# A linear-attention and low-rank mixer kernel: the order and banks of its half-size products, its x, u and kv units, and where attention stands between them

## The chip, the cores and the metric

One core of one Trainium2 chip. The metric is the device time of one execution in microseconds. In the text, TensorE (PE) multiplies, VectorE (DVE), ScalarE (ACT) and GpSimd (POOL) work on elements, and SyncE (SP) issues DMAs; POOL issues some as well.

## The reference

Eight samples of 8 heads, 576 positions and 64 features go through a linear attention; its output x (576 x 512 per sample) goes through a low-rank mixing over positions and a two-layer network.

```python
r = maximum(x, 0)                       # for q and for k, then
phi = concatenate([r * cos(theta), r * sin(theta)])        # theta by position
kv, z = einsum('bhsf,bhsd->bhfd', k_p, v), sum(k_p, axis=2)
x = einsum('bhsf,bhfd->bhsd', q_p, kv) / (einsum('bhsf,bhf->bhs', q_p, z)[..., None] + 1e-06)
h = x.transpose(0, 2, 1) @ U @ V        # rank 32, over positions
u = x + h.transpose(0, 2, 1)
out = u + maximum(u @ w_ch1, 0.0) @ w_ch2                  # 512 -> 2048 -> 512
```

## The kernel before

A sample's 576 positions are four blocks of 128 (c = 0 to 3) and a tail of 64 (c = 4); the tails of two samples share one block ("tail" units). All instructions are put in order by hand: a list `slots` holds 274 units, and a table `todo` holds what is put behind each of them, in order. Each engine works through its own instructions in that order.

The slots, for pairs of samples (even e, odd o):
- first layer: 16 units `g1_main` (L541: four matmuls of 512 columns into one of three banks tagged "g"; L550: ScalarE's relu into `hid`). Sample 0 starts at slot 0, then samples 1 to 7 at 32, 70, 100, 138, 168, 206, 236. For odd samples four `g1_tail` units (L561, L568) follow.
- second layer: for sample 0 four plain products (L601, L609). For samples 1 to 7, 14 units `w_part` (L708): seven products of half the size, each of 16 matmuls of 256 columns in two half-steps. They need sums of blocks of `hid` ("S" forms, L684: four forms, each made in two halves on VectorE, the third in place in `hid`) and of w_ch2 ("T" forms, `w2_form`, L660: eight VectorE instructions, made once). The results go into two banks, "oA" and "oB", in turns. Between them: ScalarE's cast of the first product into `w_sum` (L108), VectorE's add to it (L722), three GpSimd adds of `w_sum` and u into the output tiles `o_sb` (L722), VectorE's adds, and the stores (L575).
- behind odd samples four `g2_tail` units (L625, L634), whose output goes through the same ring of two `o_sb` buffers.

PSUM has eight banks: "g" three, "X" two (x units), "T" one, "oA" and "oB" one each.

Attention of sample b is put behind slots, relative to a slot w(b) in the table PLAN:
- features: `q_prep`, `k_prep` (L267 on VectorE, L265 on ScalarE): for each block a cos and a sin instruction, 20 per sample, all on one engine for most samples; `v_prep` (L110, GpSimd) casts v.
- `qtr_dma` (L344, L349): SyncE's transposing DMAs of q, three per sample.
- `kv_unit` (L301): 20 matmuls and a VectorE cast, twice; `x_unit` (L408): 8 matmuls, then VectorE's rec (L365, L366) and product (L418), five times, all in the two banks "X"; `A_unit` (L433, L439) with a cast on VectorE; `u_unit` (L453, L456; L460 the VectorE add), four or five times; the bank of kv, A and u is chosen by `spare`.
- `utr_dma` (L476, L482): transposing DMAs of u into uT, which the sample's first layer reads.
- `loads` of sample b + 1's q, k and v (L74, L81, L87) on SyncE, into single buffers.

```python
PLAN = {
    2: (45, -15, V_, V_, -10, (-5, -4, -4)),   # w, features at, engines for q and k, q transposes, loads
    3: (64, -11, V_, A_, -6, (7, 7, 12)),
    4: (100, -20, V_, V_, -12, (-6, -6, -6)),
    5: (134, -20, A_, A_, -13, (-7, -7, -7)),
    6: (168, -20, V_, V_, -12, (-6, -6, -6)),
    7: (202, -20, A_, A_, -13, ()),
}
```

Of the kernel before, what the change touches and what calls it, by code (L numbers as in the profile page):

```python
# [17 lines left out]
def kernel(  # L18
# [36 lines left out]
    ps = ctx.enter_context(tc.tile_pool(name="ps", bufs=1, space=bass.MemoryType.PSUM))  # L55

# [176 lines left out]
    G3, T1, OA, OB = ("g", 3), ("T", 1), ("oA", 1), ("oB", 1)  # L233
    turn = [0]

    def O2():
        turn[0] += 1
        return (OB, OA)[turn[0] % 2]

# [53 lines left out]
    def kv_unit(b, hg, tag, bufs, eng=None):  # L293
        if b not in kv_sb:
            kv_sb[b] = pool.tile([P, H, E], BF16, tag="kv", bufs=2, name="kv")
        acc = ps.tile([P, 4, E], FP32, tag=tag, bufs=bufs, name="kv_ps")
# [11 lines left out]
        cast(eng or V_, kv_sb[b][:, hg * 4 : hg * 4 + 4, :], acc)  # L308

    def qT_alloc(b):  # L310
        if b not in q_pT:
            q_pT[b] = pool.tile([P, 4, H, P], BF16, tag="q_pT", bufs=2, name="q_pT")

    def qtr_unit(b, c, h0=0, h1=H, eng=None, tag="T", bufs=1):
        qT_alloc(b)
        t_ps = ps.tile([P, H, P], BF16, tag=tag, bufs=bufs, name="t_ps")
# [51 lines left out]
    def den_unit(b, h0, h1, tag, bufs):  # L368
        n = h1 - h0
        d_ps = ps.tile([P, 5, n], FP32, tag=tag, bufs=bufs, name="d_ps")  # L370
# [12 lines left out]

    def xh_unit(b, c, h0, h1, rec, tag, bufs):
# [3 lines left out]
        acc = ps.tile([P, n, D], FP32, tag=tag, bufs=bufs, name="xh_ps")  # L388
# [12 lines left out]
    def x_unit(b, c, tag, bufs):  # L401
# [3 lines left out]
        acc = ps.tile([P, 2, 512], FP32, tag=tag, bufs=bufs, name="x_ps")  # L405
# [22 lines left out]
    def A_unit(b, tag, bufs, eng=None, n0=0, n1=DM, a_ps=None):  # L428
        if a_ps is None:
            a_ps = ps.tile([P, DM], FP32, tag=tag, bufs=bufs, name="a_ps")  # L430
# [15 lines left out]
    def u_unit(b, c, tag, bufs):  # L446
# [4 lines left out]
        va = ps.tile([P, DM], FP32, tag=tag, bufs=bufs, name="va_ps")  # L451
        if c < 4:
            nc.tensor.matmul(out=va, lhsT=V_bf[:, c, :], rhs=A_of(b), start=True, stop=True)  # L453
        else:
# [7 lines left out]
            op=ALU.add,  # L462
        )
# [22 lines left out]
    def uTd_open(b, d, tag, bufs, t=None):  # L486
        uT_alloc(b)
        if t is None:
            t = ps.tile([P, 4, P], FP32, tag=tag, bufs=bufs, name="uT_ps")
# [105 lines left out]
    def g2_part(cc, part):  # L595
        if part == 0:
            tag, bufs = G3 if cc >= 2 else O2()
            o_ps[cc] = ps.tile([P, DM], FP32, tag=tag, bufs=bufs, name="o_ps")
# [14 lines left out]
    def g2_tail(pr, part):  # L613
        last = pr == NPAIR - 1
        if part == 0 or last and part == 3:
            tag, bufs = OB if part == 0 else OA
            o_ps[pr] = ps.tile([P, DM], FP32, tag=tag, bufs=bufs, name="ot_ps")
# [34 lines left out]
    def w2_form(n, half):  # L652
# [7 lines left out]
        V_.tensor_tensor(out=T[n][:, r, :], in0=a, in1=b_, op=op)  # L660
# [25 lines left out]
    w_ps, w_sum = {}, {}  # L686

    def w_part(b, n):
        step, half = divmod(n, 2)
        if n == 0:  # L690
            w_ps[b, 0] = ps.tile([P, 2, HD], FP32, tag="oA", bufs=1, name="wa_ps")
        if n == 2:
            w_ps[b, 1] = ps.tile([P, 2, HD], FP32, tag="oB", bufs=1, name="wb_ps")
        bank = w_ps[b, step % 2]
        lhs, rhs = (
            (lambda: hid_block(b, 0, 0), w2_block(0, 0)),
            (lambda: s_forms[b, 2], T[1]),
            (lambda: hid_block(b, 1, 0), w2_block(1, 0)),
            (lambda: s_forms[b, 1], T[0]),
            (lambda: s_forms[b, 3], T[2]),  # L700
            (lambda: s_forms[b, 4], w2_block(1, 1)),
            (lambda: hid_block(b, 1, 1), T[3]),
        )[step]
        lhs = lhs()
        opens = step in (0, 1, 3, 4)
        for k_ in range(half * 4, half * 4 + 4):
            for g in range(2):
                nc.tensor.matmul(  # L708
                    out=bank[:, g, :], lhsT=lhs[:, k_, g * P : g * P + P], rhs=rhs[:, k_, :],
# [3 lines left out]
        if n < 2:  # L713
            for f in ((1, 2), (4, 3))[n]:
                hid_form(b, f, 1)
# [8 lines left out]
        if step == 0:  # L724
            w_sum[b] = pool.tile([P, 2, HD], FP32, tag="w_sum", bufs=1, name="w_sum")
            cast(A_, w_sum[b], bank)
        elif step == 1:
            w = w_sum[b]
            o0, o1 = o_alloc(b, 0), o_alloc(b, 1)
            add(V_, w, w, bank)  # L730
# [3 lines left out]
        elif step == 2:  # L734
            o0 = o_sb[b, 0]
            add(V_, o0[:, :, lo], u[:, 0:2, lo], bank)
        elif step == 3 or step == 4:
            o = o_sb[b, 1][:, :, hi]
            add(V_, o, o, bank)
        elif step == 5:  # L740
            o = o_sb[b, 0][:, :, hi]
            add(V_, o, o, bank)
            store(store_eng(b), b, 0, o_sb[b, 0])
        else:
            o = o_sb[b, 1][:, :, lo]
            add(V_, o, o, bank)
# [21 lines left out]
    def first_units(b):  # L768
        starts[b] = len(slots)
        lay([lambda j=j: g1_main(b, j) for j in range(NJ)], False)  # L770
        if b > 0:
            for i in range(4):
                beside.setdefault(starts[b] + 9 + i, []).append(
                    lambda i=i: hid_form(b, (1, 2, 4, 3)[i], 0)
                )
# [21 lines left out]
    def spare(at):  # L797
        if second[at]:
            return T1 if not all(second[at : at + 2]) else G3
        return T1 if any(second[at : at + 3]) else O2()  # L800

    QORD = (4, 0, 1, 2, 3)
    PLAN = {
        2: (45, -15, V_, V_, -10, (-5, -4, -4)),
        3: (64, -11, V_, A_, -6, (7, 7, 12)),
        4: (100, -20, V_, V_, -12, (-6, -6, -6)),
        5: (134, -20, A_, A_, -13, (-7, -7, -7)),
        6: (168, -20, V_, V_, -12, (-6, -6, -6)),
        7: (202, -20, A_, A_, -13, ()),
    }  # L810

    def attention_plan(b):

        plan = []
        w, f_at, q_eng, k_eng, qtr, lo = PLAN[b]

        def put(at, f, *a, tag=False):
            if tag:
                a = a + spare(w + at)
            plan.append((w + at, lambda: f(b, *a)))  # L820

        for n, c in enumerate(QORD):
            if b == 3:
                put(f_at + 2 * n, q_prep, c, (q_eng, q_eng))
                put(n - 8, k_prep, c, (k_eng, k_eng))
                put(-3 if n > 2 else n - 10, v_prep, 0, H, (c,), (A_ if n > 2 else G_,))
                continue
            put(f_at + n, q_prep, c, (q_eng, q_eng))
            put(f_at + 6 + n, k_prep, c, (k_eng, k_eng))
            put(f_at + 3 + (3 * n) // 2, v_prep, 0, H, (c,), (G_,))  # L830
        for n, (c0, c1) in enumerate(((4, 5), (0, 2), (2, 4))):
            put(qtr + 2 * n, qtr_dma, c0, c1)
        put(0, kv_unit, 0, tag=True)
        put(2, kv_unit, 1, tag=True)
        for n, c in enumerate(ORD):
            put(4 + 2 * n, x_unit, c, "X", 1)
        put(14, A_unit, tag=True)
        odd = b % 2 == 1
        for n, c in enumerate((4, 0, 1, 2, 3) if odd else (0, 1, 2, 3)):
            put(16 + n, u_unit, c, tag=True)  # L840
        if odd:
            put(18, utr_dma, 4, 5)
        put(18 + odd, utr_dma, 0, 2)
        put(20 + odd, utr_dma, 2, 4)
        for at, t in zip(lo, loads(b + 1) if lo else ()):
            plan.append((w + at, t))
# [16 lines left out]
    def xh_mm(b, c, h0, tag, bufs):  # L863
        acc = ps.tile([P, 4, D], FP32, tag=tag, bufs=bufs, name="xh_ps")
# [46 lines left out]
    def first_chain(b):  # L911
# [30 lines left out]
        a_ps = ps.tile([P, DM], FP32, tag=ao[0], bufs=ao[1], name="a_ps")  # L942
        a_mm(b, a_ps, 0, 256, range(5))
        cast(A_, A_of(b)[:, 0:256], a_ps[:, 0:256])
        for tag, bufs in (T1, O2()):
            t.insert(-1, ps.tile([P, 4, P], FP32, tag=tag, bufs=bufs, name="uT_ps"))
# [17 lines left out]
    for c in TL:  # L964
        tg = G3 if c < 3 else O2()
        t_q.append(ps.tile([P, H, P], BF16, tag=tg[0], bufs=tg[1], name="t_ps"))
# [69 lines left out]
    for n, c in enumerate(ORD):  # L1036
        at((32, 42, 43, 44, 45)[n], lambda c=c: u_unit(1, c, *O2()))
# [5 lines left out]
    for n in range(4):  # L1043
        for half in range(2):
            todo.setdefault(33 + 2 * n + half, []).append(
                lambda n=n, half=half: w2_form(n, half)
            )
# [44 lines left out]
```

## Time and profile before

| what | value |
|---|---|
| three runs | 341.31 us median, 338.14 to 346.68 |
| the profiled execution | 341.27 us, its span 338.8 us |
| granted TensorE clock, mean | 0.967 |
| TensorE busy | 304.1 us, 90% of the span |
| VectorE, ScalarE, GpSimd busy | 205.7, 139.5, 71.6 us |

An engine's busy time is the union of its instructions. A wait line reads "engine, line and tile that waited <- what it waited for: total us, times, longest". A window line gives the stretch, its length, the busy time and number of instructions, the granted clock as a share of full speed, the DMA engines' busy share and GB/s. A timeline line gives start, length, engine, line, operation, tiles, shapes, count, and in brackets the idle time before it.

### The profile page before, as it was taken

What the parts mean: (1) busy time and instruction counts of PE and PEld (TensorE: products, weight loads), DVE (VectorE), ACT (ScalarE), POOL (GpSimd) and SP (SyncE); (2) the same over time, 40 slices, a digit from 0 to 9 for tenths busy, and PEclk for the clock granted to TensorE, in tenths of its full rate; (3) what the DMA queues carried; (4) which work ended last, traced back from release to release, by engine and by line L of the source; (5) the groups of instructions that cost most, each with busy time, mean ns of one, the idle gap of its engine ahead of it and who ended that gap; (6) DMA issues with size and microseconds to landing.
All of it is one profiled execution on the core that took longest, in us unless ns stands there. A gap on an engine that the chain in (4) does not pass through costs nothing. (4 is left out here: it accounts for less than half of the span.)

```text
span 338.8 us, 6435 instructions
## 1 busy us (share of the span) xinstructions
PE 304.1 (90%) x2641; PEld 194.1 (57%) x2641; DVE 205.7 (61%) x419; ACT 139.5 (41%) x236; POOL 71.6 (21%) x105
## 2 busy tenths in 40 slices
PE   6999999975969499799997979779997999999995
PEld 2675455432947243585486634566466754874883
DVE  4778734998499248963863246982764357633341
ACT  3835720550580045104598035203689145127500
POOL 8500300400050105061304140051123210300030
PEclk9799999995999989899999989999999999999998
DMA  7999799689218994599239970299818510330004
GB/s 220 354 233 280 129 232 273 209 166 301 77 18 120 260 277 122 102 235 327 83 57 163 314 244 2 46 174 285 258 21 137 160 43 12 67 122 4 2 0 155
DMA packets 85279, 53.25 MB, mean 157 GB/s; under 512 B 54019, under 2 KB 82979, under 8 KB 85251
## 3 DMA queue, kind: packets, MB, share of 16 engines
q1 hardware_dynamic: 78802, 41.40, 49.7%
q0 software_dynamic: 6368, 11.43, 13.3%
q8 instruction: 20, 0.33, 0.4%
q14 instruction: 9, 0.07, 0.1%
q10 hardware_dynamic: 80, 0.03, 0.0%
HBM read 36.86 MB, written 9.44 MB: 137 GB/s over the span
## 5 line engine op out<-in xcount | busy, mean ns | idle before, releaser
L550 ACT ACTIVATE hid<-g_ps 128x512 bf16<-128x512 f32 x128 | 76.2, 597 | 140.4 <-PE g_ps L541 102.6
L541 PE MATMUL g_ps<-uT,w_bf 128*128 128x512 bf16 x512 | 125.6, 389 | 4.4 <-DMA uT<-u_bf 4.4
L541 PEld LDWEIGHTS <-w_bf 128*128 128x128 bf16 x512 | 47.9, 99 | 66.3 <-issue 14.1
L708 PEld LDWEIGHTS <-hid 128*128 128x128 bf16 x448 | 44.2, 99 | 14.4 <-issue 7.9
L722 POOL TENSOR_TENSOR o_sb<-w_sum,u_bf 128x512 f32<-128x512 f32 x21 | 26.8, 1297 | 114.2 <-DVE w_sum L722 102.8
L708 PEld LDWEIGHTS <-S 128*128 128x128 bf16 x336 | 32.8, 98 | 8.5 <-DVE S L684 2.4
L708 PE MATMUL wa_ps<-w_bf,hid 128*128 128x256 bf16 x224 | 28.7, 283 | 3.9 <-ACT w_sum L108 3.8
L110 POOL CAST v_ext<-vst 128x512 bf16<-128x512 f32 (+1 forms) x28 | 19.8, 733 | 55.7 <-DMA vst<-in_v_dram 55.7
L708 PE MATMUL wb_ps<-T,S 128*128 128x256 bf16 x224 | 27.0, 273 | 3.8 <-DVE S L684 2.1
L708 PE MATMUL wa_ps<-T,hid 128*128 128x256 bf16 x224 | 26.9, 273 | 0.4 <-DVE o_sb L722 0.3
L460 DVE TENSOR_TENSOR u_bf<-x_bf,va_ps 128x512 bf16<-128x512 bf16 x32 | 21.7, 681 | 8.8 <-PE va_ps L453 8.8
L365 DVE TENSOR_SCALAR rec<-x_ps 128x8 f32<-128x8 f32 (+1 forms) x35 | 5.7, 164 | 32.4 <-PE x_ps L408 32.4
L453 PE MATMUL va_ps<-A_sb,V_bf 128*128 128x512 bf16 x32 | 12.6, 393 | 8.8 <-DVE u_bf L460 7.8
L418 DVE TENSOR_TENSOR x_bf<-x_ps,rec 128x512 bf16<-128x512 f32 x28 | 19.4, 691 | 1.0
L110 DVE CAST kv<-kv_ps 128x260 bf16<-128x260 f32 x15 | 6.4, 428 | 18.4 <-PE kv_ps L301 18.4
L575 POOL DMA_DIRECT2D out_dram<-o_sb x12 | 7.6, 631 | 47.2 <-DVE o_sb L609 24.9
L408 PEld LDWEIGHTS <-q_pT 128*128 128x128 bf16 x224 | 10.9, 101 | 11.4 <-DMA vst<-in_v_dram 2.5
L722 DVE TENSOR_TENSOR o_sb<-o_sb,wb_ps 128x512 f32<-128x512 f32 x14 | 9.6, 686 | 12.1 <-PE wb_ps L708 11.2
L722 DVE TENSOR_TENSOR o_sb<-o_sb,wa_ps 128x512 f32<-128x512 f32 x14 | 9.6, 685 | 12.1 <-PE wa_ps L708 12.1
L684 DVE TENSOR_TENSOR S<-hid 128x1024 bf16<-128x1024 bf16 x14 | 9.5, 682 | 10.9 <-ACT hid L550 10.9
L561 PE MATMUL gt_ps<-uT_tl,w_bf 128*128 128x128 bf16 x256 | 16.1, 219 | 0.0
L561 PEld LDWEIGHTS <-w_bf 128*128 128x128 bf16 x256 | 15.1, 98 | 1.4
(143 smaller groups left out, 401.6 us busy)
## 6 DMA issues: line engine op xcount, KB each, us to landing
qst<-in_q_dram SPq DMA_DIRECT2D x14, 512.0 KB, 6.4
kst<-in_k_dram SPq DMA_DIRECT2D x14, 512.0 KB, 8.3
vst<-in_v_dram SPq DMA_DIRECT2D x12, 512.0 KB, 9.0
out_dram<-o_sb POOLq DMA_DIRECT2D x12, 512.0 KB, 7.0
w_bf<-in_moe_w_ch_dram POOLq DMA_DIRECT2D x8, 512.0 KB, 11.0
out_dram<-o_sb SPq DMA_DIRECT2D x4, 512.0 KB, 3.7
qst<-in_q_dram SPq DMA_DIRECT2D x2, 640.0 KB, 6.6
kst<-in_k_dram SPq DMA_DIRECT2D x2, 640.0 KB, 10.9
```

The costliest lines, as they stand in the source:

```text
L110: eng.tensor_copy(out=o, in_=i)
L408: nc.tensor.matmul(out=acc[:, g, i * E : i * E + E], lhsT=qT_of(b, c, h), rhs=kv_sb[b][:, h, :], start=True, stop=True,)
L418: nc.vector.tensor_tensor(out=x_of(b, c, rows).rearrange("p (g i d) -> p g i d", g=2, d=D), in0=view[:, :, :, 0:D], in1=rec[rows].unsqueez ...
L453: nc.tensor.matmul(out=va, lhsT=V_bf[:, c, :], rhs=A_of(b), start=True, stop=True)
L460: nc.vector.tensor_tensor(out=u_bf[b][:, c, :] if c < 4 else u_tl[b // 2], in0=x_of(b, c), in1=va, op=ALU.add,)
L541: nc.tensor.matmul(out=g_ps.rearrange("p (c t) -> p c t", c=4), lhsT=w1_bf[:, d, j * P : j * P + P], rhs=uT[b][:, :, d, :], start=(d == 0) ...
L550: nc.scalar.activation(out=hid[b][:, j, :], in_=g_ps, func=AF.Relu, bias=0.0, scale=1.0)
L561: nc.tensor.matmul(out=g_ps[:, jj, :], lhsT=w1_bf[:, d, j * P : j * P + P], rhs=uT_tl[pr][:, d, :], start=(d == 0), stop=(d == 3),)
L575: eng.dma_start(out=bass.AP(tensor=nines_o.tensor, offset=nines_o.offset + c * DM, ap=[[9 * DM, TS], [5 * DM, 2], [1, 2 * DM]],), in_=o.re ...
L684: V_.tensor_tensor(out=o, in0=a, in1=b_, op=op)
L708: nc.tensor.matmul(out=bank[:, g, :], lhsT=lhs[:, k_, g * P : g * P + P], rhs=rhs[:, k_, :], start=(opens and k_ == 0 and g == 0), stop=(k ...
L722: eng.tensor_tensor(out=o, in0=x, in1=y, op=ALU.add)
```

## The change

In words:
- The seven products of samples 1 to 7 go into four banks. The first and the fifth product of the new order share one bank of a new pair "O"; the second has a "g" bank; the third and sixth, and the fourth and seventh, share a "g" bank each. "oA" and "oB" are given up at slot 32, and "O" takes their two banks.
- The halves of the S forms are put elsewhere: the first halves one slot earlier, the second halves behind half-steps 0, 1, 4 and 8 (before: 0, 0, 1, 1).
- The eight T forms go from VectorE to GpSimd, at slots 18, 20, 22, 24, 29, 36, 39 and 42 (before 33 to 40).
- From sample 2 on, x units take "O" and "X" in turns, kv is one unit of 40 matmuls with one cast, u is made for two blocks at a time (`u_pair`), the cast of A is ScalarE's, and sample 1's u units take "T" and "O".
- Attention is laid out by two slots: F (features; from sample 3 on the second layer of sample b - 2) and G (kv and x; the start of sample b - 1's first layer). From sample 3 on, features go one by one, 14 to ScalarE and 6 to VectorE.

```diff
+    def kv_pair(b, tag, bufs):
+        kv_sb[b] = pool.tile([P, H, E], BF16, tag="kv", bufs=2, name="kv")
+        acc = bank([P, 2, 512], FP32, tag, bufs, "kv_ps")
...
+        cast(
+            V_, kv_sb[b].rearrange("p (g i) e -> p g (i e)", g=2), acc[:, :, 0 : 4 * E]
+        )
...
+    def u_pair(b, c, tag, bufs):
...
+        va = bank([P, 2, 512], FP32, tag, bufs, "va_ps")
+        for i in range(2):
+            nc.tensor.matmul(
+                out=va[:, i, :], lhsT=V_bf[:, c + i, :], rhs=A_of(b), start=True, stop=True
+            )
+        nc.vector.tensor_tensor(
+            out=u_bf[b][:, c : c + 2, :], in0=x_bf[b][:, c : c + 2, :], in1=va, op=ALU.add
+        )
...
-            tag, bufs = OB if part == 0 else OA
+            tag, bufs = T1 if part == 0 else O1
...
-        V_.tensor_tensor(out=T[n][:, r, :], in0=a, in1=b_, op=op)
+        G_.tensor_tensor(out=T[n][:, r, :], in0=a, in1=b_, op=op)
...
-        lhs, rhs = (
-            (lambda: hid_block(b, 0, 0), w2_block(0, 0)),
-            (lambda: s_forms[b, 2], T[1]),
-            (lambda: hid_block(b, 1, 0), w2_block(1, 0)),
-            (lambda: s_forms[b, 1], T[0]),
-            (lambda: s_forms[b, 3], T[2]),
-            (lambda: s_forms[b, 4], w2_block(1, 1)),
-            (lambda: hid_block(b, 1, 1), T[3]),
+        lhs, rhs, to = (
+            (lambda: hid_block(b, 0, 0), w2_block(0, 0), 0),
+            (lambda: s_forms[b, 2], T[1], 1),
+            (lambda: s_forms[b, 1], T[0], 2),
+            (lambda: s_forms[b, 3], T[2], 3),
+            (lambda: hid_block(b, 1, 0), w2_block(1, 0), 0),
+            (lambda: s_forms[b, 4], w2_block(1, 1), 2),
+            (lambda: hid_block(b, 1, 1), T[3], 3),
         )[step]
         lhs = lhs()
-        opens = step in (0, 1, 3, 4)
+        opens = step < 4
+        if opens and half == 0:
+            tag, bufs = O1 if to == 0 else G3
+            w_ps[to] = bank([P, DM], FP32, tag, bufs, f"w_ps{to}")
...
-        if n < 2:
-            for f in ((1, 2), (4, 3))[n]:
-                hid_form(b, f, 1)
+        for f in {0: (1,), 1: (2,), 4: (3,), 8: (4,)}.get(n, ()):
+            hid_form(b, f, 1)
...
+        ops = [(f, c, i) for f in (q_prep, k_prep) for c in QORD for i in range(2)]
+        if b == 2:
+            F, G = 30, 42
+            for n, (f, c, i) in enumerate(ops):
+                put(F + n // 2 + n // 10, feature, f, c, i, V_)
+            for n, c in enumerate(QORD):
+                put(F + 3 + (3 * n) // 2, v_prep, 0, H, (c,), (G_,))
+            at_q, at_load = (F + 5, F + 7, F + 9), (F + 10, F + 11, F + 11)
+            kv_at, x_at, a_at, u_at = 44, (46, 47, 48, 50, 51), 53, (55, 57)
+            banks = (O1, X1, O1, X1, O1)
+        else:
+            F, G = starts[b - 2] + (20 if odd else 16), starts[b - 1]
+            n = 0
+            for s_ in range(G - F):
+                for eng in (A_, V_)[: 1 + (s_ in (2, 4, 6, 8, 10, 12))]:
+                    if n < len(ops):
+                        put(F + s_, feature, *ops[n], eng)
+                    n += 1
+            V0 = starts[b - 2] + 9 if b > 3 else F - 4
+            for n, c in enumerate(QORD):
+                put(V0 + n, v_prep, 0, H, (c,), (G_,))
+            at_q, at_load = (F + 7, F + 7, F + 8), (F + 9, F + 14, V0 + 5)
+            kv_at, x_at, a_at = G, [G + i for i in (2, 4, 6, 8, 10)], G + 13
+            u_at, banks = (G + 15, G + 18), (O1, X1, O1, X1, O1)
...
+        put(a_at, A_unit, *T1, A_)
+        for n in range(2):
+            put(u_at[n], u_pair, 2 * n, *X1)
         if odd:
-            put(18, utr_dma, 4, 5)
...
+            put(u_at[1] + 1, u_unit, 4, *T1)
+        put(u_at[0] + 2, utr_dma, 0, 2)
+        put(u_at[1] + 2, utr_dma, 2, 4)
+        if odd:
+            put(u_at[1] + 3, utr_dma, 4, 5)
...
-        at((32, 42, 43, 44, 45)[n], lambda c=c: u_unit(1, c, *O2()))
+        at((33, 42, 43, 44, 45)[n], lambda c=c: u_unit(1, c, *(O1 if n % 2 else T1)))
+    at(32, pair_o)
```

More of the change, by code (lines that the diff above doesn't have):

```diff
@@ L238, in O2, with pair_o, bank @@
         return (OB, OA)[turn[0] % 2]
+    def pair_o():
+        ps_rest[0].close()
+        ps_rest[0] = ctx.enter_context(
+            tc.tile_pool(name="ps_O", bufs=1, space=bass.MemoryType.PSUM)
+        )
+    def bank(shape, dt, tag, bufs, name):
+        if tag in ("oA", "oB"):
+            return ps_o.tile(shape, dt, tag=tag, bufs=bufs, name=name)
+        if tag == "O":
+            t = ps_rest[0].tile([P, 2, 512], FP32, tag=tag, bufs=bufs, name=name)
+            return t if len(shape) == 3 else t[:, 0, :]
+        return ps.tile(shape, dt, tag=tag, bufs=bufs, name=name)
     k_p, q_p, q_pT, kv_sb, x_bf = {}, {}, {}, {}, {}
@@ L429, in A_unit @@
         if a_ps is None:
-            a_ps = ps.tile([P, DM], FP32, tag=tag, bufs=bufs, name="a_ps")
+            a_ps = bank([P, DM], FP32, tag, bufs, "a_ps")
         w = (n1 - n0) // 4
@@ L725, in w_part @@
             w_sum[b] = pool.tile([P, 2, HD], FP32, tag="w_sum", bufs=1, name="w_sum")
-            cast(A_, w_sum[b], bank)
+            cast(A_, w_sum[b], res)
         elif step == 1:
@@ L795, with feature @@
     lay_all()
[L797 to L800, printed above, removed]
     QORD = (4, 0, 1, 2, 3)
[L803 to L810, printed above, removed]
+    def feature(b, f, c, i, eng):
+        f(b, c, (eng, None) if i == 0 else (None, eng))
@@ L812, in attention_plan @@
     def attention_plan(b):
         plan = []
[L815 to L830, printed above, removed]
@@ L941, in first_chain @@
         ao = O2()
-        a_ps = ps.tile([P, DM], FP32, tag=ao[0], bufs=ao[1], name="a_ps")
+        a_ps = bank([P, DM], FP32, *ao, "a_ps")
         a_mm(b, a_ps, 0, 256, range(5))
```

110 lines of the change are left out of this document (59 added, 51 removed).

## The prediction

> **What bounds the kernel now.** I read the page's engine row first, then TensorE's waits, then the timeline around each long wait, then the clock in those windows. A "slot" is one entry of the kernel's main list.
>
> ```profile
> PE 304.1 (90%) x2641; PEld 194.1 (57%) x2641; DVE 205.7 (61%) x419; ACT 139.5 (41%) x236; POOL 71.6 (21%) x105
> ```
>
> TensorE sets the end: 90% of 338.8 us, nobody else over 61%. Its 34.7 us of idle time are what a new order can win. Its waits name the causes:
>
> ```profile
> PE va_ps L453 <- DVE u_bf L460: 7.8, 2, 5.9
> PE g_ps L541 <- DMA uT<-u_bf: 4.4, 1, 4.4
> PE wa_ps L708 <- ACT w_sum L108: 3.8, 2, 2.1
> PE wb_ps L708 <- DVE S L684: 2.1, 1, 2.1
> PE x_ps L408 <- DVE x_tl L418: 2.0, 1, 2.0
> PE x_ps L408 <- DVE x_bf L418: 2.0, 4, 1.2
> PE wb_ps L708 <- DVE w_sum L722: 1.7, 1, 1.7
> PE a_ps L433 <- DVE x_bf L418: 1.1, 2, 1.0
> PE wa_ps L708 <- DVE o_sb L722: 0.3, 1, 0.3
> ```
>
> Columns: total us, times, longest. Nearly all are PSUM banks or operands that VectorE or ScalarE hands over late. Some stalls cost twice, since TensorE runs slower behind them (TensorE's busy time, granted clock, DMA share, GB/s by window):
>
> ```profile
> 79.66:85.43 5.77, 5.77 (x35) 0.61 1.06 310
> 117.50:122.00 4.50, 4.50 (x20) 0.62 1.10 311
> 142.00:145.40 3.40, 3.40 (x19) 0.52 0.96 169
> 180.40:189.00 8.60, 8.52 (x79) 1.00 0.99 220
> 199.00:204.50 5.50, 5.50 (x32) 0.69 0.31 96
> ```
>
> Length times the missing clock: 5.77 x 0.39 = 2.25, 4.50 x 0.38 = 1.71, 3.40 x 0.48 = 1.63, 5.50 x 0.31 = 1.71 us. The fourth row follows a 2.12 us gap and lost nothing, so short gaps are sometimes free.
>
> **The ledger.** Gaps after 62 us, from TensorE's timeline, slow clock added:
> a) 73.7 to 79.66 (sample 1's u, slot 44): 5.92 + 2.25. b) 95 to 101 (sample 2's x and A): 1.25 + 0.42 + 0.97 = 2.64. c) 117.5 (uT of sample 2): 4.36 + 1.71 = 6.07. d) 141.2 (S): 2.12 + 1.63 = 3.75. e) three of 0.16 to 0.17: 0.50. f) 180.5, 258.8 (cast of w_sum): 2.12 + 1.71 = 3.83. g) 198.9 (x): 2.01 + 1.71 = 3.72. h) 216.2 (u): 1.89. i) 223.7, 225.9: 1.66 + 0.27 = 1.93. Without a: 24.33 us; with a: 32.5 us.
>
> **The change part by part.** TensorE's matmuls stay the same in number and shape, so its floor moves by nothing; everything is waits.
>
> *The products' order.* A step is 16 matmuls, 1.75 us in the chain. Before, step 3 re-uses the first step's bank after one step in between, so the cast of w_sum (0.60) and whatever ScalarE has queued ahead of it must fit into 1.75 us: f. Now three steps (5.2 us) lie between, and each other result has a bank of its own: f and i go, -5.76. The three "g" banks return to the next first layer in the order in which it takes them: the last add (0.69) is over about 1 us after the last step, its bank is wanted after two 0.86 units and a 1.20 kv pair, so this costs nothing.
>
> *x, u and kv on two pairs of banks.* x units stand two slots apart, each pair of banks has about 4 us until its next unit, against 0.17 + 0.20 + 0.69 = 1.06 of VectorE per x: b and e go but for 0.3. h goes: u pairs stand three slots (2.6 us) apart, and one pair's add takes about 1.21 (0.68 plus 512 more columns at the 0.53 by which 512 columns exceed a near-empty row). A's cast moves to ScalarE, 0.60 among 0.86 units: hidden.
>
> *Attention laid out anew.* Sample 2's u moves from slots 61 to 64 to slots 55 and 57, so its two transposes (SyncE issue 1.2 to 3.2 each, landing 1.3 to 5.1 later) start 10 slots or more before slot 70: c goes. Twenty features of a sample, 0.40 each on VectorE in a row, are replaced from sample 3 on by 6 on VectorE and 14 on ScalarE (0.62 apart), one or two per slot behind the products: d goes. ScalarE's 14 x 0.62 + 0.60 = 9.3 us fit into 14 half-steps of 0.87 = 12.2 us; without that cover the next hid evacuations would be late by the overhang. SyncE: a transposed q is issued after the odd sample's two uT. Counting from the first half-step of sample 2 or 4: second u pair added at 4.5, uT 1.2 to 3.2, u_tl 1.3, q tail 1.2, q 2.0 to 3.5: the first q half lands at 15.5 to 16.6, wanted at 18.8. Loads now wait behind these, but a sample's q and k are wanted a whole 30 us stage later.
>
> *g.* VectorE's tail add waited there for the previous output's store:
>
> ```profile
> 196.89 0.69 DVE L634 TENSOR_TENSOR o_sb<-u_tl,ot_ps 128x512 f32<-128x512 bf16 x1 [3.25 <-PE g_ps L541]
> ```
>
> The store landed at 196.77 by the DMA record, 7.4 us after its issue (2.4 to 7.7 elsewhere). That wait stays, and kv's cast now stands behind it. The second x bank takes the 2.0 us away; I leave 0.7 in all for samples 1 and 3 (0 if the store lands in 4 us; 3 each if in 7.4).
>
> *What it costs.* First, behind an odd sample's u pair (1.21) the second halves of S1 and S2 (0.60 each) are ready some 3.3 us after the last first-layer unit and wanted after 0.43 + 3 x 0.87 = 3.05: 0.25 x 3 = 0.75. Second, the eight w2 forms go from VectorE (8 x 0.60 = 4.8) to GpSimd. No row shows this form there. Nearest: its two-input add of 512 columns, 1.15 undisturbed, so 2.3 for 1024; the one-input cast (0.61 for 512) bounds it at 1.2 below, two adds in a busy stretch (1.33) at 2.7 above; I take 2.3, being a two-input operation too. The first four run at 44 to 54 us, beside VectorE work that reads PSUM, whose rows do not change beside GpSimd (0.691 either way). The last four, with five casts, 12 us, fall into 60 to 76 us, where VectorE has 20 features and S forms. There the trace shows a lock-out in both directions:
>
> ```profile
> 63.82 2.84 POOL L110 CAST v_ext<-vst 64x512 bf16<-64x512 f32 x5
> 64.21 2.73 DVE L267 TENSOR_SCALAR q_p<-qst,cosw 128x512 bf16<-128x512 f32 x1
> 98.28 1.38 DVE L267 TENSOR_SCALAR q_p<-qst,sinw 128x512 bf16<-128x512 f32 x1
> 223.73 4.75 POOL L722 TENSOR_TENSOR o_sb<-w_sum,u_bf 128x512 f32<-128x512 f32 x3 [20.61 <-DVE w_sum L722]
> ```
>
> A 0.47 feature took 2.73, ending with the fifth cast; GpSimd's first add took 2.51 instead of 1.15 behind VectorE's features. So I add the two, from 61.4 on: features 20 x 0.40 = 8.0, three S forms 1.9, GpSimd the rest of a form 1.4, casts 2.9, two forms 4.6, together 18.8, then u's add 0.68: it ends near 81 instead of 79.61, the last form taken as later. Stall a grows by 1.4 (bounds: nothing locked, 75.3, a gain of 4.3; the last form and VectorE's two PSUM reads in line as well, 84, a loss of 4.4).
> [...]
> Third, two S forms that used to come before GpSimd's three adds into o_sb (3.4 us) now come after w_sum's add, beside them. S3's second half is free at once in odd samples; with a u add between (samples 1, 2, 4, 6) GpSimd gets in first. At 98.28 VectorE waited for one add, not for all. So 0.7 for each of these four for S3 and S4, nothing more than a little for the others: 2.8 in all (0 to 2.1 per sample).
>
> **Sum.** -24.33 + 0.3 = -24.0; + 1.4 + 0.75 + 2.8 + 0.7 = 5.65: -18.4 us. The profiled execution took 341.27 us (span 338.8, the rest around it), the median of the three runs is 341.31, so both give 323 us.
>
> **The rivals.**
> 1. *GpSimd does not get in the way.* Then a shrinks to 1.6 us (u's add at 75.3) and, like the 2.12 us gap at 178.4, leaves the clock alone: 4.3 + 2.25 more, and 0.75 at most remains: 341.3 - 24.0 - 6.55 + 0.75 + 0.7 = 312. For: 13 of 14 features beside GpSimd took under 1.4. Against: the 2.73.
> 2. *SyncE's chain is too slow.* q's transposes now have 2 to 3 us to spare in samples 4 and 6 where they had 16. With the longest times seen (uT 3.24, u_tl 1.8, q tail 1.44, q 3.47, landing 8.3) the first half lands at 22.8, 4.0 late, plus 1.7 of slow clock as at c; 2 x 5.7 = 11.4 us: 334.4. Against: those maxima came in the stretch from 102 to 117 us with stores and transposes together, not one after the other.
> [...]
>
> **How the numbers follow.** Forecast 0.56, rival 1 0.20, rival 2 0.13, rival 3 0.11. All stalls gone would be 341.3 - 32.5 = 309, rounded up to 310 for the low end; the high end 337 takes in rival 2 and leaves out rival 3. About 2% is what a measurement of this kernel can tell from no change: 334.5 and 348. Faster by more: the first two and a quarter of rival 2, 0.79; within: the rest of rival 2 and half of rival 3, 0.15; slower by more: the other half of rival 3, 0.06.
>
> **What would show it.** TensorE's waits without w_sum, x_bf and uT, and idle under 15 us; one long gap near 74 us, followed by a low clock; GpSimd's forms at 2.3 us; VectorE features of over 1 us between 61 and 77 us; S waits of under 1 us in the products. I am wrong if first-layer or product units wait for DMA, if g_ps waits for an add, or if the gap near 74 us is below 3 or above 11 us.

## The result, and the profile after

The changed kernel takes 318.52 us (median of four runs, 318.18 to 320.01; the record lists a fifth, 321.98, that the median leaves out) against 342.22 for the kernel before (338.14 to 346.68): ratio 0.937, 95% interval 0.927 to 0.947. Ratios rest on a kernel's fast runs: one that is over 1.5% above its fastest counts in the median and the range, but not in the ratio. Its profiled execution took 320.01 us, span 318.1 us, mean granted clock 0.983 (before: 341.27, 338.8, 0.967). In its profile L587 is the first layer, L753 and L766 the products and their adds, L442 x, L487 a single u unit's matmul and L494 its add, L655 and L680 the adds of sample 0's and of the tails' outputs, L285 a feature on VectorE, L114 a cast, L706 a T form, L730 an S form; where an experiment adds lines, these numbers move by up to 12, and experiment 4 has those of the kernel before. The engine row of the page:

```profile
PE 295.4 (93%) x2641; PEld 191.1 (60%) x2641; DVE 200.6 (63%) x367; ACT 155.0 (49%) x260; POOL 87.2 (27%) x115
```

TensorE executes as many matmuls as before. Of the 20.7 us that the span lost, 12.0 are idle time (338.8 - 304.1 = 34.7 before, 318.1 - 295.4 = 22.7 now), and 8.7 are busy time, most of it work that no longer runs at half clock: 7.3 behind stalls by the ledger and 1.7 at the start (half of a 3.41 us stretch) before, 2.05 now, so 7.0; the other 1.7 I can't place. Some 1.5 us of the whole is chance: the first kv matmul came at 15.77 us instead of 17.29, in a stretch that the change leaves alone. From there to the end it is 321.5 against 302.3 us; this "inner time" is used below, where the start would blur a comparison.

TensorE's waits behind its first 16 us (total us, times, longest):

```profile
PE va_ps L487 <- DVE u_bf L494: 6.8, 1, 6.8
PE va_ps L487 <- DVE u_tl L494: 3.4, 1, 3.4
PE x_ps L442 <- DVE kv L114: 2.1, 1, 2.1
PE w_ps L753 <- DVE x_bf L452: 1.2, 1, 1.2
PE w_ps L753 <- DVE S L730: 0.4, 1, 0.4
PE w_ps L753 <- DVE hid L730: 0.3, 2, 0.2
PE g_ps L587 <- DVE o_sb L655: 0.3, 1, 0.3
```

The waits for uT, the cast of w_sum, x_tl and A are gone. One stall remains, and it has grown: sample 1's u, 10.2 us in two parts, with one u unit and four first-layer matmuls between them, against 5.9. The clock around it and behind it:

```profile
74.29:81.12 6.83, 0.00 (x1) 0.00 (x0) 6.80 (x16) 0.60 (x1) 0.00 (x0) 0.55 0.91 167
81.12:85.23 4.11, 4.11 (x35) 2.46 (x35) 1.93 (x3) 0.60 (x1) 0.00 (x0) 0.50 0.88 206
142.00:180.00 38.00, 38.00 (x361) 26.34 (x359) 22.69 (x41) 22.14 (x36) 9.56 (x12) 1.00 0.87 205
```

In the first row TensorE does nothing while VectorE is busy for all of it (third number 6.80); in the second it works at half clock. The third, a stretch of 38 us without a gap, ran at full clock. Before, five stretches were at half clock ahead of the last matmul, one at the start among them; now it is this one. The half-clock stretches here are multiples of 3.41 us: 10.24 from 74.99 us on, that is three; before, 3.41 four times and 6.83 once. The stall at 186 us, 2.08 long, left the clock at 1.00.

The stall's cause stands in the timeline of VectorE and GpSimd (start, length, engine, line):

```profile
59.18 1.53 DVE L285 TENSOR_SCALAR q_tl<-qst,cosw 64x512 bf16<-64x512 f32 x1
62.42 9.59 DVE L285 TENSOR_SCALAR q_p<-qst,cosw 128x512 bf16<-128x512 f32 x1
72.33 0.67 DVE L494 TENSOR_TENSOR u_tl<-x_tl,va_ps 128x512 bf16<-128x512 bf16 x1
80.39 0.68 DVE L494 TENSOR_TENSOR u_bf<-x_bf,va_ps 128x512 bf16<-128x512 bf16 x1
...
58.28 2.14 POOL L706 TENSOR_TENSOR T<-w_bf 128x1024 bf16<-128x1024 bf16 x1
62.65 1.17 POOL L114 CAST v_ext<-vst 64x512 bf16<-64x512 f32 x2
63.79 2.11 POOL L706 TENSOR_TENSOR T<-w_bf,T 128x1024 bf16<-128x1024 bf16 x1
69.62 2.10 POOL L706 TENSOR_TENSOR T<-w_bf,T 128x1024 bf16<-128x1024 bf16 x1
```

One feature of 0.47 us took 9.59. GpSimd did five casts and three T forms without a pause from 62.65 to 71.72 us, and the feature ended 0.28 us after the last. In experiments 3, 5, 6, 9 and 10, which leave these instructions in their order, the same feature takes 9.58 to 9.60 us, and TensorE's wait for u_tl behind it is 3.4 us in each. The u add that opens the way for sample 1's third u unit came at 80.39. TensorE's side of the two parts:

```profile
73.05 0.38 PE L487 MATMUL va_ps<-A_sb,V_bf 128*128 128x512 bf16 x1 [3.37 <-DVE u_tl L494]
81.12 0.59 PE L487 MATMUL va_ps<-A_sb,V_bf 128*128 128x512 bf16 x1 [6.83 <-DVE u_bf L494]
```

Each unit waits for the add of the one just before it. So sample 1's u units do not take "T" and "O" in turns, as the description of the change has it: the lambda in that line of the diff reads `n` only when it runs, and by then a later loop (`for n, t in enumerate(loads(2))`) has left `n` at 2, so that all five ask for "T", of which there is one. By turns, TensorE could have done one u unit and four first-layer matmuls more before it stood, some 1.2 us (an estimate, from 73.05 to 74.29 here); no run tries it.

### The profile page after: what moved, and what is told of

It is laid out like the page before. It is cut to its first block, busy times and chain, and to the rows that moved or that the text cites. A ratio compares the mean times of both kernels' runs of the same rounds, so it can differ in the third digit from the quotient of the medians.

```text
span 318.1 us, 6434 instructions
## 1 busy us (share of the span) xinstructions
PE 295.4 (93%) x2641; PEld 191.1 (60%) x2641; DVE 200.6 (63%) x367; ACT 155.0 (49%) x260; POOL 87.2 (27%) x115
## 4 chain that ended last, share of the span: by engine, by line
PE 77%; DVE 15%; DMA 5%; issue 2%; ACT 0%; DVEq 0%; ACTq 0%
PE g_ps L587 31%; PE w_ps L753 22%; DVE q_p L285 5%; PE gt_ps L607 4%; PE o_ps L647 4%; PE ot_ps L671 3%; PE x_ps L442 3%; DMA out_dram<-o_sb 3%; PE kv_ps L335 2%; DMA qst<-in_q_dram 2%; DVE k_p L285 2%; PE va_ps L504 1%; DVE o_sb L766 1%; DVE S L730 1%; DVE hid L730 1%
## 5 line engine op out<-in xcount | busy, mean ns | idle before, releaser
L587 PE MATMUL g_ps<-uT,w_bf 128*128 128x512 bf16 x512 | 120.9, 381 | 0.3 <-DVE o_sb L655 0.3
L587 PEld LDWEIGHTS <-w_bf 128*128 128x128 bf16 x512 | 47.5, 98 | 62.3 <-issue 13.4
L766 POOL TENSOR_TENSOR o_sb<-w_sum,u_bf 128x512 f32<-128x512 f32 x21 | 27.9, 1353 | 119.6 <-DVE w_sum L766 119.6
L753 PEld LDWEIGHTS <-hid 128*128 128x128 bf16 x448 | 43.4, 98 | 8.0 <-DVE x_bf L452 1.3
L753 PEld LDWEIGHTS <-S 128*128 128x128 bf16 x336 | 32.3, 98 | 6.9 <-DVE S L730 1.5
L753 PE MATMUL w_ps<-w_bf,hid 128*128 128x256 bf16 x224 | 26.8, 273 | 1.2 <-DVE x_bf L452 1.2
L507 DVE TENSOR_TENSOR u_bf<-x_bf,va_ps 128x1024 bf16<-128x1024 bf16 x12 | 14.6, 1219 | 20.4 <-PE va_ps L504 20.4
L753 PE MATMUL w_ps<-T,hid 128*128 128x256 bf16 x224 | 27.1, 273 | 0.3 <-DVE hid L730 0.3
L753 PE MATMUL w_ps<-T,S 128*128 128x256 bf16 x224 | 26.8, 273 | 0.0
L766 DVE TENSOR_TENSOR o_sb<-o_sb,w_ps 128x512 f32<-128x512 f32 x28 | 19.1, 682 | 9.8 <-PE w_ps L753 8.4
L114 POOL CAST v_ext<-vst 128x512 bf16<-128x512 f32 (+1 forms) x30 | 17.6, 624 | 25.0 <-DMA vst<-in_v_dram 24.8
L285 DVE TENSOR_SCALAR q_p<-qst,cosw 128x512 bf16<-128x512 f32 x17 | 21.5, 1281 | 3.3 <-DMA qst<-in_q_dram 3.3
L730 DVE TENSOR_TENSOR S<-hid 128x1024 bf16<-128x1024 bf16 x14 | 9.6, 688 | 12.8 <-ACT hid L596 12.8
L647 PE MATMUL o_ps<-w_bf,hid 128*128 128x512 bf16 x64 | 15.6, 379 | 0.0
L283 ACT ACTIVATE k_p<-kst,sinw 128x512 bf16<-128x512 f32 x22 | 15.0, 714 | 0.1
L671 PE MATMUL ot_ps<-w_bf,hid_tl 128*128 128x512 bf16 (+2 forms) x80 | 14.5, 336 | 0.0
## 6 DMA issues: line engine op xcount, KB each, us to landing
w_bf<-in_moe_w_ch_dram POOLq DMA_DIRECT2D x8, 512.0 KB, 11.3
kst<-in_k_dram SPq DMA_DIRECT2D x2, 640.0 KB, 11.3
```

The lines of the kernel that those rows point to most:

```text
L114: eng.tensor_copy(out=o, in_=i)
L283: nc.scalar.activation(out=o, in_=i, func=AF.Relu, bias=0.0, scale=w)
L285: eng.tensor_scalar(out=o, in0=i, scalar1=0.0, scalar2=w, op0=ALU.max, op1=ALU.mult)
L587: nc.tensor.matmul(out=g_ps.rearrange("p (c t) -> p c t", c=4), lhsT=w1_bf[:, d, j * P : j * P + P], rhs=uT[b][:, :, d, :], start=(d == 0) ...
L647: nc.tensor.matmul(out=o, lhsT=hid[0][:, j, cc * P : cc * P + P], rhs=w2_bf[:, j, :], start=(j == 0), stop=(j == NJ - 1),)
L671: nc.tensor.matmul(out=o[:, cols], lhsT=hid_tl[pr][:, j, :], rhs=w2_bf[:, j, cols], start=(j == 0), stop=(j == NJ - 1),)
```

## The experiments

My theory after this result: the stall at sample 1's u is VectorE's lateness behind GpSimd's run, and the rest of the gain is the removal of the listed waits. What had to be told apart was which edit removed which wait. Ratios are to the kernel before on the same chip.

**1. T forms back on VectorE.**

```diff
-        G_.tensor_tensor(out=T[n][:, r, :], in0=a, in1=b_, op=op)
+        V_.tensor_tensor(out=T[n][:, r, :], in0=a, in1=b_, op=op)
```

> The changed kernel with the eight T forms on VectorE again, in the slots that the change gave them. Theory 1 (GpSimd's long run of forms and casts shut VectorE out, 9.59 us at 62.4 us of the changed kernel's trace): no feature of sample 2 takes over about 2.9 us (the five casts alone), VectorE's own work up to u's first add is then 8.0 + 1.2 + 2.4 of forms + 1.9 of S + at most 2.3 behind the casts, so that the add ends near 75 to 76 us instead of 81; TensorE's gaps near 73 and 81 us (3.4 + 6.8) shrink to 2 to 4 us in all; time 310 to 314 us. Rival (VectorE was overloaded there in any case, and the forms only come on top of it): the gaps stay over 8 us, time 318 to 322 us.

Measured: 313.91 us (311.96 to 317.23), ratio 0.916 (0.907 to 0.925). The stall is one gap of 5.1 us (in the trace, of the execution of 317.23 us). The longest feature is 3.35 us, behind the five casts alone:

```profile
63.35 3.35 DVE L285 TENSOR_SCALAR q_p<-qst,cosw 128x512 bf16<-128x512 f32 x1
```

So the move of the T forms to GpSimd made this stall longer, by 5.1 us, though VectorE now has 8 x 0.68 us more to do. The gap is above the 2 to 4 us that I expected: the casts still hold VectorE for 2.9.

**2. T forms on GpSimd, but all eight in slots 18 to 28.**

```diff
-        todo.setdefault((18, 20, 22, 24, 29, 36, 39, 42)[i], []).append(
+        todo.setdefault((18, 20, 22, 24, 25, 26, 27, 28)[i], []).append(
```

> The changed kernel with the last four T forms still on GpSimd, but straight behind the first four (slots 25 to 28 instead of 29, 36, 39 and 42), ahead of GpSimd's first store and of sample 2's features. Theory 1: the forms run from about 52 to 60.5 us beside VectorE work that reads PSUM, VectorE loses at most 1.5 us at its first feature and some 2.3 us behind the five casts, its load is 2.4 us less than with the forms on VectorE: gaps of 1 to 3 us in place of 10.2, time 308 to 312 us. Rival (the place of the forms does not matter, GpSimd's total time does): gaps over 8 us, time 318 to 322 us.

Measured: 312.94 us (311.5 to 314.95), ratio 0.916 (0.908 to 0.923). GpSimd's forms of 2.12 us run from 43.05 to 59.98 us, and no feature or S form lay beside them until 59.67; the casts come after, and hold one feature:

```profile
62.11 3.34 DVE L285 TENSOR_SCALAR q_p<-qst,cosw 128x512 bf16<-128x512 f32 x1
...
57.86 2.12 POOL L706 TENSOR_TENSOR T<-w_bf,T 128x1024 bf16<-128x1024 bf16 x1
62.32 2.84 POOL L114 CAST v_ext<-vst 64x512 bf16<-64x512 f32 x5
```

The gap is 3.65 us, and time and gap are a little above what I expected (308 to 312, 1 to 3). The same engine with the same work, earlier, costs nothing that shows against experiment 1. It is the place that was wrong, not the engine.

**3. The old order of the products in the new layout.** Line added in `w_part`:

```diff
+        step = (0, 1, 4, 2, 3, 5, 6)[step]
```

> The changed kernel with the seven products in the order of the kernel before (the one that adds onto the first product's bank comes third, one product after it, not fifth), on the new banks. Theory A (the new order took away the waits for the cast of w_sum, 1.7 to 2.1 us each at samples 3 and 5): such waits come back in TensorE's list, about 2 us in two to six samples, time 322 to 330 us. Theory B (ScalarE now has one feature per slot in its queue, so that the cast is done at most 0.62 + 0.6 us after its product, inside the 1.75 us of the product between): no wait for w_sum over 0.3 us, time within 1 us of the changed kernel, 317 to 320 us.

Measured: 323.12 us (320.97 to 324.06), ratio 0.944 (0.936 to 0.952). No wait for the cast of w_sum came back, so theory A is out; the median is above theory B's range as well. There is a new wait, 2.0 us over three samples:

```profile
PE w_ps L754 <- DVE o_sb L767: 2.0, 3, 0.7
```

A bank is taken again there with one product between, and VectorE's add is not done. The profiled span is 321.0 us, but its first kv matmul came 3.4 us later than in the changed kernel; the inner times are 301.9 and 302.3 us. By the waits the order is worth about 1 us inside the new layout (2.0 here against 0.9 for S and hid), by the inner time nothing, by the medians 4.6 with intervals that meet: small, and its size not settled.

**4. The new order and banks alone, in the kernel before.** `w_part` as after the change, with "oA" for the first and fifth product and three "g" banks for the others; attention's kv, A and u units inside the products use bank "T" alone, since products hold the "g" banks there; everything else, the S halves too, as before.

> The kernel before with nothing but the new order of the products and a bank for each of the four running sums (one of the two o banks and the three g banks); attention's A, kv and u units inside the products use bank T. Theory A: the waits for w_sum and for its add (3.8 + 1.7 + 0.3 us in TensorE's list) are gone, 335 to 337 us. Theory B: ScalarE's queue of features still holds the cast back, but three products (5.2 us) cover it, so that the waits go as well here; the two theories agree on this kernel, and it measures what the order is worth with the old attention: 5.8 us at most. Rival: the T bank in place of two makes kv and u units wait, and nothing is won, 340 to 343 us.

Measured: 331.4 us (330.34 to 334.68), ratio 0.971 (0.962 to 0.980); the inner time is 310.2 against 321.5, 11.3 us less, about twice the 5.76 that the ledger credits to f and i and more than I expected (335 to 337 us). The waits for w_sum are gone, and the one bank "T" brings some of the rival's waits (0.73 and 0.87 us at 105 and 109 us); what else changed lies at other entries of the ledger:

```profile
PE va_ps L453 <- DVE u_bf L460: 8.9, 3, 5.9
PE g_ps L541 <- DMA uT<-u_bf: 1.1, 1, 1.1
PE w_ps L707 <- DVE S L684: 2.1, 1, 2.1
```

The uT wait of sample 2 fell from 4.36 to 1.1. The 2.1 for S stays, and the 5.9 at sample 1's u, but no half-clock stretch follows c or d any more: two stretches of 3.41 us fewer are 3.4 us (the mean granted clock is 0.979, before 0.967). Gains of the parts don't add: alone the order is worth 11 us, on top of the rest about 1.

**5. Each sample's features on one engine again.**

```diff
-                        put(F + s_, feature, *ops[n], eng)
+                        one = A_ if odd else V_
+                        if b == 3:
+                            one = V_ if n < 10 else A_
+                        put(F + s_, feature, *ops[n], one)
```

> The changed kernel with the features of samples 3 to 7 again on one engine per sample, as before the change (odd samples ScalarE, even ones VectorE, sample 3 half and half). Theory 1 (splitting each sample's features over both engines took the waits for S and the late VectorE adds away): a wait of TensorE for S, u or a product bank comes back in samples 4 and 6, where VectorE gets all twenty, 1.5 to 2.5 us each, and the time rises by 3 to 6 us, to 321 to 325. Theory 2 (the split does nothing, the other S halves and the pairs removed those waits): within 1.5 us of 318.5, no single new gap over 0.5 us.

Measured: 331.04 us (330.76 to 333.22), ratio 0.975 (0.969 to 0.981): the largest single loss of all the parts undone. It is theory 1, with over twice the loss that it expected. TensorE's waits:

```profile
PE w_ps L753 <- DVE S L730: 4.9, 3, 2.1
PE w_ps L753 <- DVE hid L730: 4.2, 3, 1.9
PE kv_ps L335 <- DVE k_p L285: 2.9, 4, 1.2
```

They fall at 102 to 109, 142 to 153 and 215 to 226 us: the products beside which VectorE has ten features (the first stretch) or all twenty (the others) of the next sample between the S forms. Besides S, kv waits for the last features, which I had not expected. The gap of 2.14 us near 108 is followed by 3.41 us at half clock, as d was.

**6. All x units in the banks X.**

```diff
-            banks = (O1, X1, O1, X1, O1)
+            banks = (X1,) * 5
```

(also in `u_at, banks` for the later samples).

> The changed kernel with every x unit of the samples from the third on in the one pair of banks X, instead of by turns in O and X. Theory 1 (the turns between two pairs are worth what the ledger gave x units, and cost 1.2 us in sample 2, where the first product needs O right behind the last x unit): the 1.2-us gap near 94 us goes, in its place come waits of 0.2 to 0.5 us in front of x units, and the time stays within 1.5 us of 318.5. Theory 2 (without the turns the x units wait for the whole evacuation again): waits of 1.5 to 2 us return at the x units of two samples or more, and the time is 322 to 326.

Measured: 320.21 us (318.46 to 321.5), ratio 0.943 (0.937 to 0.949); inner time 301.1 against 302.3. The 1.2 us gap is gone, and sample 2's x units wait 0.42, 0.33 and 0.33 us instead:

```profile
PE x_ps L442 <- DVE x_bf L452: 0.7, 2, 0.3
PE x_ps L442 <- DVE x_tl L452: 0.4, 1, 0.4
```

Theory 1, though the median is 0.2 us beyond its 1.5. The two-pair turns are worth 1.1 us and cost 1.2; the later samples' x units, two slots apart, show no gap over 0.1 us with one pair.

**7. A version without the causes found:** all T forms in slots 18 to 28; sample 2's v casts on VectorE, and five of its q features on ScalarE; its x units in the order X, O, X, O, X; a buffer of its own for the tail outputs.

```diff
-        todo.setdefault((18, 20, 22, 24, 29, 36, 39, 42)[i], []).append(
+        todo.setdefault((18, 20, 22, 24, 25, 26, 27, 28)[i], []).append(
...
-                put(F + n // 2 + n // 10, feature, f, c, i, V_)
+                if n < 10 and i == 1:
+                    put(27 + n // 6, feature, f, c, i, A_)
+                else:
+                    put(F + n // 2 + n // 10, feature, f, c, i, V_)
...
-                put(F + 3 + (3 * n) // 2, v_prep, 0, H, (c,), (G_,))
+                put(F + 9 + n // 2, v_prep, 0, H, (c,), (V_,))
...
-            banks = (O1, X1, O1, X1, O1)
+            banks = (X1, O1, X1, O1, X1)
...
+            if b >= B:
+                o_sb[b, r] = pool.tile([P, 1, DM], FP32, tag="o_tl", bufs=1, name="o_tl")
...
```

> The changed kernel with four edits: all eight T forms in slots 18 to 28 (as in the run with early forms), sample 2's five v casts on VectorE in place of GpSimd and five of its q features on ScalarE, sample 2's x units in the order X, O, X, O, X, and a buffer of its own for the tail outputs. Theory 1 (the gap at sample 1's u is VectorE's lateness alone, the gap near 94 us is the bank O of the last x unit, the tail add waits for a store's buffer): against the run with early forms (312.9) the gap near 74 us shrinks from 3.6 to 0 to 1.5 us, the half-clock stretch after it goes (1.7 us), the 1.2-us gap falls under 0.4, and the wait for the tail add's buffer is gone in every run: 306 to 309.5. Theory 2 (u's first evacuation is late for another reason, its matmuls or the transposes): the gap near 74 us stays above 2.5 us and the time stays at 310.5 or more.

Measured: 310.41 us (305.91 to 312.6), ratio 0.903 (0.895 to 0.911), the best of all, though its interval meets that of experiment 2. Inner time 288.4 (experiment 2: 294.3).

```profile
PE va_ps L487 <- DVE u_bf L494: 1.3, 1, 1.3
PE w_ps L756 <- DVE S L733: 1.0, 1, 1.0
```

And the tail add of sample 3 in VectorE's timeline:

```profile
170.18 0.69 DVE L683 TENSOR_TENSOR o_tl<-u_tl,ot_ps 128x512 f32<-128x512 bf16 x1 [2.70 <-PE ot_ps L674]
```

The stall at u is 1.34 us, inside the expected 0 to 1.5, with no half-clock stretch behind it (granted clock 1.00 from 73.3 to 150 us). The gap near 94 is gone (a wait of 0.95 for S at 96 us has come up from 0.35), and the tail add waits for TensorE alone. The four runs took 305.91, 308.23, 312.58 and 312.60 us: the median is 1 us above the expected range, the mean of the two that the ratio rests on, 307.07, inside it. In the profiled one, 308.23, TensorE had 3.41 us at half clock at the start (mean granted clock 0.994), outside all that the edits touch.

**8. GpSimd's run broken up.** Six copies of one column, each waiting for one of VectorE's features, between GpSimd's casts and forms:

```diff
+    def hold(src, c):
+        G_.tensor_copy(out=mark3, in_=src[2][:, c, 0, D : D + 1])
...
```

> The changed kernel with six one-column copies on GpSimd, each of which waits for one of VectorE's features, put between GpSimd's casts and T forms of 62 to 72 us, so that GpSimd pauses after one or two of its instructions. Theory 1 (VectorE's feature is held by an unbroken run of such GpSimd instructions, to its end): no feature takes over 3.5 us, where one took 9.59; several take 1 to 3; the held time in all stays about the same, so the first u add stays within 2 us of 80.4 us and the gap there at 8 to 12 us in all. Theory 2 (something else holds that one feature, its data or a transfer): one feature still takes over 6 us.

Measured: one run, 316.52 us, span 314.4, inner time 299.0.

```profile
66.94 2.36 DVE L295 TENSOR_SCALAR k_tl<-kst,cosw 64x512 bf16<-64x512 f32 x1
73.33 2.33 DVE L295 TENSOR_SCALAR k_p<-kst,cosw 128x512 bf16<-128x512 f32 x1
77.60 0.68 DVE L504 TENSOR_TENSOR u_bf<-x_bf,va_ps 128x512 bf16<-128x512 bf16 x1
...
71.64 3.74 POOL L718 TENSOR_TENSOR T<-w_bf 128x1024 bf16<-128x1024 bf16 x1
```

No feature takes over 2.36 us, so theory 2 is out: the long hold is GpSimd's run, and not the feature's own data. Of theory 1, that the hold lasts to the end of a run is not shown: the feature at 66.94 ended 0.28 us behind one form, though GpSimd went straight on to a copy and two casts. The held time did not quite stay the same either: the u add came 2.8 us earlier and the two gaps there are 7.35 us, not 8 to 12. One T form took 3.74 instead of 2.11, while VectorE did four instructions in a row: here GpSimd was held beside VectorE.

**9. Single u units.**

```diff
-        for n in range(2):
-            put(u_at[n], u_pair, 2 * n, *X1)
+        for n in range(4):
+            put(u_at[0] + n, u_unit, n, *X1)
```

> The changed kernel with the u units of the samples from the third on one column block at a time again, four single units in the pair of banks X in four slots that follow each other, in place of two pairs. Theory 1 (the pairs took the waits for u and for its transposes away): each single unit has to wait for the add of the one before, 0.3 to 0.8 us each, and the last transposes start late, so that a wait of 1 to 4 us for uT comes back in one sample or more: 321 to 327. Theory 2 (the earlier places alone did it): at most 0.3 us of waits per sample, 317 to 320.5.

Measured: 321.92 us (320.84 to 322.39), ratio 0.947 (0.941 to 0.953); inner time 302.2, the same as with pairs.

```profile
PE va_ps L487 <- DVE u_bf L494: 8.4, 4, 6.8
```

Of this, 6.8 is the old stall; the single units added 1.54 us of waits, all in sample 2 between 100 and 104 us, and no wait for uT. By the median it is 3 us slower, by the inner time not at all: what pairs are worth is between nothing and that. The uT wait did not need them; that the earlier places took it away is left as the reading, not tried by itself.

**10. The second halves of the S forms at their old places.**

```diff
-        for f in {0: (1,), 1: (2,), 4: (3,), 8: (4,)}.get(n, ()):
+        for f in {0: (1, 2), 1: (4, 3)}.get(n, ()):
```

> The changed kernel with the second halves of the S forms issued as before the change, two behind each of the first two half products. Theory 1 (spreading them took the wait for S away): VectorE works through four forms in a row ahead of the adds that open the way for the products, and waits of 0.5 to 2 us for S or a bank come back in several samples: 320.5 to 325. Theory 2 (the features' split did it, not the places of the halves): no new wait over 0.5 us, 317 to 320.

Measured: 319.59 us (318.42 to 323.25), ratio 0.939 (0.930 to 0.948): theory 2. No wait for S or hid is left in this run, where the changed kernel has five, of 0.9 us in all. That the wait for S (d) went is the features' split (experiment 5), not the places of the second halves.

## Why the prediction came out right, and where its terms were off

The forecast was 323 us, a gain of 18.4; the profiled executions differ by 21.3, the medians by 23.7. Its mechanism, stalls of the ledger taken away with the one at sample 1's u left and longer, is what the traces show; the terms that were off partly cancel, and the gain is larger than they make it, in part by luck at the start.

- *b to i, -24.33 + 0.3*: the waits at c, d, e (as x and a waits), f, h and i are gone, and at b 1.22 us remain instead of 0.3. This is a wait I did not see coming: sample 2's last x unit is in "O" at slot 51, the first product follows at once, and opens its bank there before the x product has been read. Experiments 6 and 7 remove it by another bank.
- *Which edit earns it* was partly misread. I gave 5.76 to the products' order; alone it earns 11.3, inside the layout about 1 by the waits (experiments 4, 3). I gave d to the features' placing, which is right and larger than written: undoing it costs 11.4 us of inner time (experiment 5). I gave h to the pairs: single units bring 1.54 us of waits at other places, not h's 1.89 back (experiment 9).
- *a, +1.4*: mis-sized. The stall grew by 4.3 us (10.2 against 5.92), close to the upper bound of 4.4. The GpSimd forms took 2.12, close to the 2.3 taken. That the first u add ended at 81.07, as forecast near 81, is luck: from VectorE's first feature to the end of that add it took 21.9 us (59.18 to 81.07), where my sum has 19.5 (61.4 to 80.9) and the kernel before 18.2, but the whole began 2.2 us earlier; in experiment 3, whose start was late, the same 21.9 us ended at 84.22. The term that failed is the last form, which I took as later: it ran inside the hold (69.62 to 71.72), 2.1 us more, as in my upper bound. And the stall begins earlier than I took it: u_tl's add stands behind the held feature as well, and its bank "T" is the one that the next unit asks for, so that TensorE waits from 69.7 us on and not from near 74. The half-clock loss behind is 4.11 x 0.50 = 2.05, like before.
- *S2 at 0.75*: nothing; no such wait is in the trace. *S3 and S4 at 2.8*: 0.35 + 0.16 + 0.13 + 0.16 + 0.13 = 0.9. GpSimd's adds gave way at each boundary, as I read from the row at 98.28:

```profile
135.41 1.28 DVE L730 TENSOR_TENSOR hid<-hid 128x1024 bf16<-128x1024 bf16 x1
136.61 1.38 DVE L285 TENSOR_SCALAR q_p<-qst,cosw 128x512 bf16<-128x512 f32 x1
...
134.98 4.02 POOL L766 TENSOR_TENSOR o_sb<-w_sum,u_bf 128x512 f32<-128x512 f32 x3 [16.24 <-DVE w_sum L766]
```

  Two VectorE instructions got in during three adds.
- *g, 0.7*: 2.08, in sample 3 alone. The mechanism is the one given, kv's cast behind a tail add that waits for a store; the store took 8.5 us to land (176.16 to 184.68), longer than the 7.4 that I priced:

```profile
184.80 0.69 DVE L680 TENSOR_TENSOR o_sb<-u_tl,ot_ps 128x512 f32<-128x512 bf16 x1 [7.20 <-DMA out_dram<-o_sb]
```

  In the eight experiments on the changed kernel that keep the two buffers, this wait is 0 to 2.06 us (seven of them 0.43 or more, 0.78 in the middle), so 0.7 was a fair size and 2.08 is the upper end.

- *The sum* with the measured sizes is 24.33 - 1.22 - 4.1 - 0.9 - 2.1 = 16.0 us, less than the 18.4 forecast. Of the 5.3 us up to 21.3, 1.5 are luck at the start, 0.8 a wait at 33 us (a u unit for q_pT) that stood in no term and is gone, and some 3 I can't place (the 1.7 above among them).
- *What would show it*: no w_sum and no uT wait, right; an x_bf wait, but of a product; idle from 61 us to the last matmul 14.7, under the 15 set; the gap near 74 us 10.2 in all, under the 11. One sign of being wrong did occur, in small: g_ps waits for an add, 0.29 us at 61.5. It is the add of sample 0's output, and it stood behind the feature of 1.53 us at 59.18, which ran beside a T form.
- *The rivals*: rival 1 (312) did not come from GpSimd staying out of the way, yet experiment 2 reaches its 312.9 by giving GpSimd its forms where nothing collides. Rival 2 has no wait for DMA in the products or the first layer. Rival 3 (by my estimate 345 us, at 0.11) took GpSimd to keep VectorE out through all three of its adds into `o_sb`, for 3.4 us in each of samples 1 to 6. No run shows that: two VectorE instructions got in during the adds at 134.98 us, and the waits for S and hid are 0.9 us in all. A long hold there was, 9.59 us, but behind casts and T forms.

## What to carry to other kernels

Before work is moved to GpSimd, look at which VectorE instructions will run beside it: here those that read and write SBUF only were held (a feature of 0.47 us for 9.59), those that read PSUM were not (x's products took 0.69 us beside the early forms, as elsewhere), and the same eight forms cost 5 us or nothing depending on their slots. Put a ledger line to an edit only when it has been undone by itself: the order of the products earned 11 us alone and about 1 behind the other edits. A bank chosen in a lambda by a loop's variable is chosen when the lambda runs; look in the trace for which unit waits for which. Where TensorE sets the end, a handover that is about 2 us late costs its wait and, behind some of these gaps here, 3.41 us at half clock on top (the last section lists them).

## What the runs showed of the hardware

- A feature of 0.47 us on VectorE was held for 9.59 us, through eight GpSimd instructions back to back; with pauses between them the longest was 2.36 (experiment 8). The feature began 0.23 us ahead of the first cast (62.42 and 62.65 us) and was passed over at seven boundaries, so here the one that began first was not done first, and the hold did not end with one GpSimd instruction. GpSimd's three f32 adds at 134.98 us did give way at each boundary, and in experiment 8 so did one pair of casts (at 69.29 us; the features beside it took 0.85 and 0.82) and a form with a one-column copy behind it (at 66.63). Why these do and the forms and casts in the long run do not stays open.
- The other way round, a T form of 2.11 us on GpSimd took 3.74 us beside four VectorE instructions in a row (experiment 8, at 71.64 us).
- The T form, two inputs and 1024 columns in bf16, takes 2.12 us on GpSimd (experiment 2, and 43.62 us after the change) and 0.68 on VectorE (experiment 1 and before).
- Gaps of TensorE of 2.0 to 2.2 us had 3.41 us at half clock behind them in some places and none in others. With it: before, the gaps of 2.12 that ended at 141.23 us and of 2.01 at 198.89, and in experiment 5 the one of 2.14 near 108. Without: before, 2.12 at 180.48, and after the change 2.08 at 186.15. In these two kernels' profiles no gap under 1.9 us from 60 us on had one.
